# Attention and MLP in one kernel: merged exps and mask products, global rows added up by TensorE, and one opening order in place of two

## The chip, the cores and the metric

The kernel runs on one core of one Trainium2 chip. The metric is the device time of one execution in microseconds. Five engines work side by side, each through its own instructions in program order: TensorE (PE, matmuls; PEld, its weight loads), VectorE (DVE), ScalarE (ACT), GpSimd (POOL) and SyncE (SP). Matmul results go to PSUM, eight banks of 2 KB a partition. GpSimd and SyncE start the transfers (DMAs).

## The reference, cut to what matters

```python
def _attn_ref(q, k, v, global_idx):            # 8 batches, 8 heads, 576 tokens, head size 64
    scores = scale * np.matmul(q, k.transpose(0, 1, 3, 2))
    mask = np.abs(pos[:, None] - pos[None, :]) <= 32       # a band of 65
    mask = mask | is_global[:, None] | is_global[None, :]  # 8 global tokens
    attn = softmax(np.where(mask, scores, -1e9))
    return np.matmul(attn, v)

def _moe_ref(x, w_in, w_out):                  # 4608 tokens, 512 wide, 2048 inner
    h = x @ w_in
    g = h * np.cos(h)
    return g @ w_out
```

The attention's output, heads side by side, is x of the second part.

## The kernel before

**The work.** Heads go in pairs: 32 pairs, four to a batch of 576 tokens. A pair is worked off in steps, each a letter and the pair's number. *k* and *q* turn the natural rows of keys and queries with 16 small TensorE transposes (L618) and copy them to SBUF on ScalarE (L627, L638, L639); pairs 0 to 3 also pick the global columns with 16 matmuls (L323, copied at L324), and from pair 2 on the q step issues two filler matmuls first (L613). *s*, the scores, are ten matmuls (L654) into four PSUM banks, exps on ScalarE (L657, L661) and products with the mask on VectorE (L658, L662). *p*, the values, are 20 matmuls (L669) into the tile pv, then on VectorE the sum of the global rows' denominators (L683), two reciprocals (L684, L685) and the product xn (L689). *x* turns xn back with five transposes (L701) into xT, the MLP's input (L702, L705, L707); the last pair of a batch also has GpSimd copy the eight global columns to places held in registers (L710).

Pairs 0 to 9 go by five blocks of 120 tokens as above (scores5, values5, turn_x5); from pair 10 on another layout with eleven blocks is used (L722 to L775), with keys and queries cast to a 16-bit copy in DRAM and read back by a transposing DMA.

The MLP goes by nine tiles of 512 tokens. mlp_in makes one of 16 column blocks of h in four matmuls (L788), then a cos on ScalarE (L794) and a product on VectorE (L795); mlp_out adds four of its blocks into the output (L892); the last three tiles use a form with seven products in place of eight (L852). exp and cos need different function tables, so ScalarE loads a table whenever it changes between them.

**The order** is written out by hand in strings, one token a step. FRONT is the start, MID what follows it, then one string for each two pairs (FIFTH, SIXTH, ORDER) and TAIL. `1` is an mlp_in with its cos, `m` one without, `t` a cos alone, `2` an mlp_out. `w4` are four filler matmuls (L330) and `f8` eight (L514). GpSimd's queue has: `L` load of keys and queries of four heads (L290), `W` one of four chunks of w_in (L993), `O` w_out (L997), `C` cast of four heads' values (L423), `E` and `A` gathers of the global rows (L346), `H` turning them, `g` copying them into a pair's keys and queries (L598, L605), `I` the iotas and the loads of the eight positions into registers (L1045 to L1048), `K` the casts to DRAM (L277, L281). SyncE's queue has `M`, the loads of four heads' values (L384, L389), and `B`, the transposing reads (L295, L296). `y` makes the values' global rows (L430, copied at L431), `n` squares an output for a check (L914), `Z` is a part of the second layout's mask (L446 to L480), `N` holds GpSimd's queue until the mask is there. `+` and `-` say whether mlp_in may use the score banks. L1 stands for pairs 2 and 3, L2 for 4 and 5, and so on; so do C and M.

**PSUM.** pv has two banks, tag h two (turned rows, mlp_in), tag s three (scores, turned outputs), tag o one (the fourth score bank, mlp_out).

Of the kernel before, what the change touches and what calls it, by code (L numbers as in the profile page):

```python
# [53 lines left out]
MID = ("+ 1 1 1 1 Z0 1 1 1 Z5 B5 1 Z1 1 1 Z2 1 1 A0 1 Z3 1 1 A1 1 n0 A2 g10 g11 1 Z4 N K6 1 1 1 1 1 1 1 2 2 kc qc n1 2 2 1 1 B6 2 2 n2 kd qd - 2 2")  # L54
# [5 lines left out]
FRONT = ("M1 s0 E0 C0 E1 L2 w6 k1 q1 L3 w4 s1 M2 M3 y0.0 f8 k2 q2 C1 H0 I p0 y0.1 s2 k3 q3 x0 p1 H1 s3 g4 g5 g6 L4 C2 g7 k4 q4 x1 p2 M4 s4 "  # L60
         "k5 q5 x2 p3 s5 g8 g9 C3 W0 W1 W2 W3 k6 q6 x3 p4 s6 C4 k7 q7 x4 p5 s7 k8 q8 x5 p6 s8 H2 O k9 q9 p7 x6 s9 "
         "x7 p8 m m x8 K5 p9 t t + m m t t x9 -")
# [149 lines left out]
def kernel(  # L212
# [28 lines left out]
    gidx_row = const.tile([1, 2 * G], I32)  # L241
# [4 lines left out]
    nc.sync.dma_start(gidx_row, dview(gi, 0, (2 * G, 1), (1, 2 * G)))  # L246
# [7 lines left out]
    xT = keep.tile([P, NC, NT + 40], FP16)  # L254

# [70 lines left out]
    def warm(n, tag="s"):  # L326

        t = ps.tile([P, 4, P], FP32, tag=tag, bufs=2 + (tag == "s"))
        for _ in range(n):
            nc.tensor.matmul(t, ones16, view(ones16, (0, 4), (1, P)), start=True, stop=True)  # L330
# [76 lines left out]

    def hold_mask(_):

        nc.gpsimd.tensor_copy(gate, mask[0:1, 0, 0:1])  # L410
# [8 lines left out]
    def cast_vn(s):  # L419
        if s == 2:  # L420
            nc.gpsimd.tensor_copy(gate, pm_of[max(pm_of)][0:1, 2 * CN - 1 : 2 * CN])
# [3 lines left out]
    def value_rows(s, part):  # L425

        hs = slice(2 * part, 2 * part + 2)
        rows = ps.tile([P, 512], FP32, tag="h", bufs=2, name="rows")
# [143 lines left out]
    def turn_globals(half, both):  # L572
        t = ps.tile([P, 2, 16 * G], FP16, tag="s" if half else "h", bufs=2 + half)
# [35 lines left out]
    def turned(src, pr, n, ahead=0):  # L609

        bank = ps.tile([P, 512], FP32, tag="h", bufs=2, name="bank")
        for _ in range(ahead):
            nc.tensor.matmul(bank, ones16, view(ones16, (0, 4), (1, P)), start=True, stop=True)  # L613
        t = view(bank.bitcast(FP16), (QP, RW), (1, QP))
# [4 lines left out]
        return t, bank[:, 400 : 400 + G]  # L619
# [24 lines left out]
    def scores5(pr):  # L644
        kp, qp = k5(pr), qb[pr % NK].rearrange("p j c -> p (j c)")
        pm = pm_of[pr] = work.tile([P, 2 * CN], FP16, tag="pm", name="pm")
        tags = (("s", 3), ("s", 3), ("s", 3), ("o", 1))
        st = [ps.tile([P, 512], FP32, tag=tag, bufs=bufs, name="st") for tag, bufs in tags]
        for t in (0, 1, 4, 2, 3):
            i, c = (0, OFF[t]) if OFF[t] < CA else (2, OFF[t] - CA)  # L650
            q0 = 0 if t == 0 else P * t - D
            for h in range(2):
                hp = slice(h * D, (h + 1) * D)
                nc.tensor.matmul(st[i + h][:, c : c + WID[t]], kp[hp, t], qp[hp, q0 : q0 + WID[t]], start=True, stop=True)  # L654
        for h in range(2):
            e = work.tile([P, 2 * CB], FP16, tag="e", bufs=3)
            nc.scalar.activation(e[:, 0:CA], st[h][:, 0:CA], AF.Exp, scale=scale)  # L657
            nc.vector.tensor_tensor(pm[:, h * CN : h * CN + CA], e[:, 0:CA], mask5[:, 0:CA], ALU.mult)  # L658
        e = work.tile([P, 2 * CB], FP16, tag="e", bufs=3)
        for h in range(2):  # L660
            nc.scalar.activation(e[:, h * CB : (h + 1) * CB], st[2 + h][:, 0:CB], AF.Exp, scale=scale)  # L661
        nc.vector.tensor_tensor(view(pm[:, CA:], (CN, 2), (1, CB)), view(e, (CB, 2), (1, CB)), view(mask5[:, CA:], (0, 2), (1, CB)), ALU.mult)  # L662

    def values5(pr):
# [13 lines left out]
        for h in range(2):  # L678
            add(h, 0, P, G, 1, 0, False, True)
        den = pv[:, :, D : D + 1]  # L680
        rp = r_all[:, pr]
        dg = work.tile([G, 2], FP32, tag="dg")
        nc.vector.tensor_reduce(dg, view(pv[0:G, :, X + D : X + D + 1], (512, 2), (X, 4)), AX.X, ALU.add)  # L683
        nc.vector.reciprocal(view(rp, (NK5, 2), (1, NK5)), view(den, (512, 2), (X, NK5)))  # L684
        nc.vector.reciprocal(view(rp[0:G, 1:], (NK5, 2), (1, 4)), view(dg, (1, 2), (0, 4)))  # L685
# [508 lines left out]
```

## Time and profile before

| what | value |
|---|---|
| time, median of 3 runs | 336.7 us (336.4 to 339.61) |
| span of the profiled execution | 335.3 us |
| the profiled execution's own time | not listed beside its span |
| TensorE busy | 322.3 us (96%) |
| VectorE, ScalarE, GpSimd busy | 269.7, 241.1, 107.6 us |
| pair 10's scores begin (end of FRONT and MID) | 82.78 us |

The span is counted from the first to the last instruction. In the rows of the profile a line starts with the start and the length in us, then the engine, the line of the kernel, the operation, output <- inputs, shapes and a count; in brackets stands how long the engine had been idle and what released it. Grouped rows have busy us and mean ns after the bar.

### The profile page before, as it was taken

The numbers are of one execution on the slowest core, as the hardware profiler recorded it, in microseconds if no ns is written. First come the engines' busy times: TensorE is split into PE (matmuls) and PEld (weight loads), VectorE is DVE, ScalarE is ACT, GpSimd is POOL, SyncE is SP. The second block draws the span as 40 slices with busy tenths as digits, with TensorE's granted clock in tenths as the row PEclk, the third lists the DMA queues.
The fourth block names the chain that finished last, engine by engine and source line by source line (L and its number), as shares of the span: only waits on it lengthen the run. The fifth ranks groups of instructions, "written<-read, shape, count | busy, mean of one in ns | idle before, by whom it ended". The sixth has DMA issues, their size and how long they took to land.

```text
span 335.3 us, 8640 instructions
## 1 busy us (share of the span) xinstructions
PE 322.3 (96%) x3269; PEld 180.1 (54%) x3269; DVE 269.7 (80%) x649; ACT 241.1 (72%) x422; POOL 107.6 (32%) x216
## 2 busy tenths in 40 slices
PE   7999889999999999999999999999999999999992
PEld 3566654444545454545454545454545566666781
DVE  6778889984679798989898989898989878778771
ACT  4788886785958887777778787878787865665710
POOL 7856578361071407241623252325000200000000
PEclk9999999999999999999999999999999999999997
DMA  5999899999999999999999999999990010100212
GB/s 72 213 179 208 152 205 199 194 133 164 138 179 153 150 161 145 201 155 170 147 195 147 164 149 183 135 178 141 194 109 34 32 33 31 65 32 0 96 47 88
DMA packets 167220, 45.01 MB, mean 134 GB/s; under 512 B 153108, under 2 KB 163732, under 8 KB 166996
## 3 DMA queue, kind: packets, MB, share of 16 engines
q1 hardware_dynamic: 107556, 26.73, 55.9%
q0 software_dynamic: 59472, 17.54, 51.0%
q8 instruction: 27, 0.44, 0.6%
q14 instruction: 21, 0.17, 0.2%
q10 hardware_dynamic: 144, 0.13, 0.1%
HBM read 44.93 MB, written 19.17 MB: 191 GB/s over the span
## 4 chain that ended last, share of the span: by engine, by line
PE 84%; DVE 7%; ACT 5%; issue 2%; ACTq 0%; DVEq 0%
PE ph L788 29%; PE po L892 23%; PE wx L852 6%; PE wy L852 5%; PE units L788 4%; PE pv L742 3%; PE t L330 3%; PE st L722 3%; DVE g L795 2%; PE pv L669 2%; PE tx L767 2%; PE bank L618 2%; PE st L654 1%; ACT cos L794 1%; PE bank L613 1%
## 5 line engine op out<-in xcount | busy, mean ns | idle before, releaser
L788 PE MATMUL ph<-xT,w_in 128*128 128x512 f16 x512 | 123.3, 379 | 0.5 <-DVE xg L707 0.2
L794 ACT ACTIVATE cos<-ph,pio 128x512 f16<-128x512 f32 x128 | 86.5, 687 | 41.5 <-PE ph L788 39.4
L795 DVE TENSOR_TENSOR g<-cos,ph 128x512 f16<-128x512 f16 x128 | 85.6, 684 | 17.9 <-ACT cos L794 15.9
L892 PE MATMUL po<-w_out,g 128*128 128x512 f16 x384 | 93.5, 379 | 0.0
L788 PEld LDWEIGHTS <-w_in 128*128 128x128 f16 x576 | 53.8, 98 | 57.7 <-issue 1.5
L892 PEld LDWEIGHTS <-g 128*128 128x128 f16 x384 | 36.6, 98 | 43.1
L725 ACT ACTIVATE e<-st 128x512 f16<-128x512 f32 x44 | 23.9, 594 | 8.2 <-PE st L722 8.1
L726 DVE TENSOR_TENSOR pm<-e,mask 128x512 f16<-128x512 f16 x44 | 18.8, 428 | 13.4 <-ACT e L725 12.1
L1079 POOL COPY gate<-xn 1x1 f16<-1x1 f16 x8 | 1.4, 179 | 81.0 <-DVE xn L753 81.0
L775 POOL COPY xT<-xg 128x4 f16 x48 | 15.8, 328 | 32.2 <-DVE xT L770 29.6
L281 POOL DMA_DIRECT2D q<-in_q_dram x11 | 24.3, 2206 | 0.0
L753 DVE TENSOR_TENSOR xn<-pv,r_all 128x768 f16<-128x768 f32 x22 | 21.1, 958 | 0.7
L852 PEld LDWEIGHTS <-g 128*128 128x128 f16 x192 | 18.7, 98 | 5.2
L914 ACT ACTIVATE xn<-xn 128x1536 f16<-128x1536 f16 (+1 forms) x15 | 21.2, 1411 | 0.0
L281 POOL DMA_DIRECT2D k<-in_k_dram x11 | 18.0, 1638 | 1.4 <-issue 1.4
L794 ACT ACTIVATE cos<-units,pio 128x512 f16<-128x512 f32 x16 | 11.0, 689 | 9.8 <-PE units L788 9.6
L795 DVE TENSOR_TENSOR g<-cos,units 128x512 f16<-128x512 f16 x16 | 11.0, 686 | 7.4 <-ACT cos L794 7.3
L788 PE MATMUL units<-xT,w_in 128*128 128x512 f16 x64 | 16.4, 379 | 0.0
L794 ACT ACT_TABLE_LOAD x12 | 15.4, 1283 | 0.2
L600 POOL COPY kw<-kgT 128x88 f16<-128x88 f16 x22 | 14.6, 884 | 0.0
L725 ACT ACT_TABLE_LOAD x11 | 14.1, 1283 | 0.2
L722 PEld LDWEIGHTS <-kw 64*128 64x128 f16 x484 | 8.4, 95 | 10.2 <-issue 8.4
(215 smaller groups left out, 500.1 us busy)
## 6 DMA issues: line engine op xcount, KB each, us to landing
out_dram<-o SPq DMA_DIRECT2D x24, 256.0 KB
vw<-v SPq DMA_DIRECT2D x32, 165.0 KB
k<-in_k_dram POOLq DMA_DIRECT2D x11, 288.0 KB, 8.1
q<-in_q_dram POOLq DMA_DIRECT2D x11, 288.0 KB, 11.0
v<-in_v_dram POOLq DMA_DIRECT2D x11, 288.0 KB, 5.4
vn<-in_v_dram SPq DMA_DIRECT2D x20, 120.0 KB
w_in<-in_moe_w_in_dram POOLq DMA_DIRECT2D x4, 512.0 KB, 10.1
w_out<-in_moe_w_out_dram POOLq DMA_DIRECT2D x1, 2048.0 KB, 17.8
```

The lines of the kernel that those rows point to most:

```text
L281: nc.gpsimd.dma_start(dst[s].rearrange("t (h d) -> t h d", h=4), dview(src, base, (D, S), (S * D, 4), (1, D)))
L722: nc.tensor.matmul(st[j // 8 * 2 + h][:, j % 8 * C : j % 8 * C + C], kp[hp, j], qp[hp, j], start=True, stop=True)
L725: nc.scalar.activation(e[:, 0:512], st[h], AF.Exp, scale=scale)
L726: nc.vector.tensor_tensor(view(pm[:, h], (1, 512)), e[:, 0:512], view(mask, (1, 512)), ALU.mult)
L753: nc.vector.tensor_tensor(view(xn, (384, 2), (D, 6), (1, D)), view(pv, (512, 2), (65, 6), (1, D)), view(rp, (6, 2), (1, 6), (0, D)), ALU.mult)
L775: nc.gpsimd.tensor_copy(xT[:, :, bass.ds(pool_idx[g] + b * S, 1)], xg[:, :, g : g + 1])
L788: nc.tensor.matmul(ph, w_in16[:, j, f * P : (f + 1) * P], xT[:, j, t * TT : (t + 1) * TT], start=(j == 0), stop=(j == NC - 1))
L794: nc.scalar.activation(cos, ph, AF.Sin, bias=pio2)
L795: nc.vector.tensor_tensor(g, cos, ph, ALU.mult)
L852: nc.tensor.matmul(bank[:, a], left(f)[:, a * P : a * P + P], right(f), start=name in "125" and f == 0 and (split or a == 0), stop=f == HF ...
L892: nc.tensor.matmul(po, g16[:, f, s * P : (s + 1) * P], w_out16[:, f], start=(f == 0), stop=(f == NF - 1))
L914: nc.scalar.activation(view(xn, (BP * P, 2), (1, n)), view(xn, (BP * P, 2), (1, n)), AF.Square, accum_out=x_sq[:, s : s + 1])
```

## The change

- In pairs 0 to 9 the scores of both heads go to the two banks of one double tile; one exp and one mask product take both heads. Four exps become two, three products two. The four score banks are two double tiles until `F` in the order, then three banks s and one o as before; any step that asks for an s or o bank before `F` takes a whole double tile.
- values5 adds the global rows of all blocks into one place with eight small matmuls (8 rows each) instead of two, so the sum of denominators and the second reciprocal go, and the sum in turn_x5 becomes a copy.
- FRONT and MID become one string, OPEN. k is turned earlier than its q in many pairs, ahead of the scores of the pair before. The register loads and mask parts Z0 to Z4 stand at the start, the later gathers A0 to A2 and w_in chunks 1 and 0 among the first pairs, chunks 2 and 3 about pairs 5 and 6; the last two value products and four outputs stand among the mlp_in. The filler matmuls are 13 + 4 + 2 + 4, before 13 + 4 + 4 + 6 + 4. The counts of `1` with `m` (30) and `2` (8) are the same.
- The registers are loaded from gidx_all, so gidx_row and its transfer go. A few tiles share room; `finish_check` gains a memset; cos takes its bias as a constant.

```diff
-FRONT = ("M1 s0 E0 C0 E1 L2 w6 k1 q1 L3 w4 s1 M2 M3 y0.0 f8 k2 q2 C1 H0 I p0 y0.1 s2 k3 q3 x0 p1 H1 s3 g4 g5 g6 L4 C2 g7 k4 q4 x1 p2 M4 s4 "
-         "k5 q5 x2 p3 s5 g8 g9 C3 W0 W1 W2 W3 k6 q6 x3 p4 s6 C4 k7 q7 x4 p5 s7 k8 q8 x5 p6 s8 H2 O k9 q9 p7 x6 s9 "
-         "x7 p8 m m x8 K5 p9 t t + m m t t x9 -")
-MID = ("+ 1 1 1 1 Z0 1 1 1 Z5 B5 1 Z1 1 1 Z2 1 1 A0 1 Z3 1 1 A1 1 n0 A2 g10 g11 1 Z4 N K6 1 1 1 1 1 1 1 2 2 kc qc n1 2 2 1 1 B6 2 2 n2 kd qd - 2 2")
+OPEN = ("w2 M1 I Z0 R1 E0 C0 E1 L2 Z1 M2 k1 Z2 H2 M3 s0 P0 f8 Z3 q1 s1 Z4 k2 y0.0 w4 W1 C1 H0 k3 L3 q2 p0 - A0 y0.1 "
+        "s2 q3 x0 W0 p1 s3 H1 R2 k4 g4 g7 p2 g6 q4 k5 p3 g5 x1 s4 A1 Q8 C2 L4 q5 g8 k6 M4 A2 x2.1 s5 g9 W2 q6 C3 x3 "
+        "W3 p4 s6 q7 g10 k7 + x4.1 O C4 K5 p5 k8 s7 g11 k9 q8 p6 x5.1 q9 s8 p7 s9 n0 m F m K6 x6.1 Z5 1 t 1 p8 1 1 1 "
+        "1 1 B5 1 x7.1 1 p9 1 2 t 1 N0 1 n1 + m t 2 1 1 2 x8.1 1 k10 1 m n2 2 1 q10 2 2 k11 1 1 q11 1 t 1 1 1 2 x9 1 "
+        "1 B6 2 1 -")
...
+    def two_banks():
+
+        return rooms[1].tile([P, 2, 512], FP32, tag="a", bufs=2, name="two")
...
 def scores5(pr):
-        tags = (("s", 3), ("s", 3), ("s", 3), ("o", 1))
-        st = [ps.tile([P, 512], FP32, tag=tag, bufs=bufs, name="st") for tag, bufs in tags]
+        both = front[0]
+        st = [two_banks(), two_banks()] if both else [[bank("s") for _ in range(2)], [bank("s"), bank("h")]]
...
-        for h in range(2):
-            e = work.tile([P, 2 * CB], FP16, tag="e", bufs=3)
-            nc.scalar.activation(e[:, 0:CA], st[h][:, 0:CA], AF.Exp, scale=scale)
-            nc.vector.tensor_tensor(pm[:, h * CN : h * CN + CA], e[:, 0:CA], mask5[:, 0:CA], ALU.mult)
...
+        for i, c, n in ((0, 0, CA), (1, CA, CB)):
+            e = work.tile([P, 2 * CA], FP16, tag="e", bufs=3)
+            if both:
+                nc.scalar.activation(view(e, (n, 2), (1, n)), st[i][:, :, 0:n], AF.Exp, scale=scale)
...
+            nc.vector.tensor_tensor(view(pm[:, c:], (CN, 2), (1, n)), view(e, (n, 2), (1, n)), view(mask5[:, c:], (0, 2), (1, n)), ALU.mult)
 def values5(pr):
-        for h in range(2):
-            add(h, 0, P, G, 1, 0, False, True)
+        for t in (4, 2, 3, 0):
+            for h in range(2):
+                add(h, t, D if t else P, G, 1, 0, False, t == 0)
...
-        dg = work.tile([G, 2], FP32, tag="dg")
-        nc.vector.tensor_reduce(dg, view(pv[0:G, :, X + D : X + D + 1], (512, 2), (X, 4)), AX.X, ALU.add)
         nc.vector.reciprocal(view(rp, (NK5, 2), (1, NK5)), view(den, (512, 2), (X, NK5)))
-        nc.vector.reciprocal(view(rp[0:G, 1:], (NK5, 2), (1, 4)), view(dg, (1, 2), (0, 4)))
 def turn_x5(pr, tag="s"):
-            nc.vector.tensor_reduce(xg[:, p], view(tx[:, 1], (1, G), (P, 4)), AX.X, ALU.add)
+        nc.vector.tensor_copy(xg[:, p], tx[:, 1, 0:G])
...
         build_mask5()
         local_k(0)
-        warm(4)
         local_q(0)
         warm(4)
...
-                gidx_row[0:1, 0 : 2 * G : 2], engines=[mybir.EngineType.Pool], min_val=0, max_val=S - 1)[1])
+                gidx_all[0:1, 0 : 2 * G : 2], engines=[mybir.EngineType.Pool], min_val=0, max_val=S - 1)[1])
```

In OPEN, `R` says how many MLP tiles may be begun, `Q` how many mlp_out may be issued, `P0` holds GpSimd's queue until pair 0's product is there, `x4.1` takes a double tile (after `F` an s bank) for the turned output instead of an h bank.

140 lines of the change are left out of this document (79 added, 61 removed).

## The prediction

> **What bounds the kernel now.** First the page's part 1, then busy time in windows cut at 45.4 (ninth pair scored), 82.8 (pair 10 scored, where the hand-written opening ends) and 104 us.
>
> ```profile
> PE 322.3 (96%) x3269; PEld 180.1 (54%) x3269; DVE 269.7 (80%) x649; ACT 241.1 (72%) x422; POOL 107.6 (32%) x216
> 7.40:45.40 38.00, 35.47 (x798) 24.89 (x797) 30.56 (x105) 30.44 (x77) 26.56 (x49) 1.00 1.12 191
> 45.40:82.80 37.40, 36.55 (x209) 17.04 (x211) 31.12 (x81) 26.93 (x41) 19.17 (x31) 1.00 1.50 177
> 104.00:252.00 148.00, 148.00 (x1470) 75.12 (x1469) 127.94 (x282) 116.39 (x192) 47.40 (x96) 1.00 1.49 159
> ```
>
> The columns are busy us and count of TensorE, its weight loads, VectorE, ScalarE and GpSimd, then the granted clock, the DMA share and GB/s. From 104 to 252 us TensorE is busy for 148.00 of 148.00. The steps there stay, so a gain must make pair 10's scores start before 82.78. What TensorE does until then:
>
> ```profile
> 8.03 1.04 PE L330 MATMUL t<-ones 128*128 128x512 f16 x4
> 9.00 0.47 PE L618 MATMUL bank<-ident,room 76*64 76x76 f16 x16
> 9.30 0.39 PE L323 MATMUL bank<-one_q,room 76*64 76x8 f16 x16
> 9.63 1.04 PE L330 MATMUL t<-ones 128*128 128x512 f16 x4
> 10.61 0.55 PE L654 MATMUL st<-qb,kw 64*128 64x136 f16 x10
> ...
> 14.75 0.55 PE L654 MATMUL st<-qb,kw 64*128 64x136 f16 x10
> ...
> 26.51 1.03 PE L669 MATMUL pv<-vw,pm 128*128 128x65 f16 x20
> 27.48 0.55 PE L654 MATMUL st<-qb,kw 64*128 64x136 f16 x10
> 27.95 0.47 PE L618 MATMUL bank<-ident,w_out 75*64 75x75 f16 x16
> 28.36 0.61 PE L613 MATMUL bank<-ones 128*128 128x512 f16 x2
> 28.89 0.47 PE L618 MATMUL bank<-ident,w_out 76*64 76x76 f16 x16
> 29.29 0.45 PE L701 MATMUL tx<-ident,xn 128*128 128x128 f16 x5
> 29.58 1.03 PE L669 MATMUL pv<-vw,pm 128*128 128x65 f16 x20
> 30.99 0.55 PE L654 MATMUL st<-qb,kw 64*128 64x136 f16 x10 [0.38 <-issue]
> ...
> 44.84 0.55 PE L654 MATMUL st<-qb,kw 64*128 64x136 f16 x10 [0.19 <-ACT qb L639]
> ...
> 52.90 21.31 PE L788 MATMUL ph<-xT,w_in 128*128 128x512 f16 x96
> 74.05 3.62 PE L892 MATMUL po<-w_out,g 128*128 128x512 f16 x16
> ...
> 82.78 0.41 PE L722 MATMUL st<-qb,kw 64*128 64x64 f16 x16
> ```
>
> Start to start a pair costs: values 0.97, scores 0.47, k turned 0.41, two fillers 0.53, q turned 0.40, output turned 0.29. Pairs 0 to 3 add a pick of 0.33 to k and to q (9.30 to 9.63). A group of four MLP matmuls takes 21.15/24 = 0.88. A filler of L330 takes (10.61-9.63)/4 = 0.24.
>
> Work from 7.40 to the ninth score's end at 45.33: 20 turnings 8.1, picks 2.6, 16 fillers of L613 4.2, scores 4.7, eight value products 7.8, seven outputs 2.0, 18 fillers of L330 4.4 and about 1.8 of small things (value rows, fill, globals): 35.6. **2.3 us are waits.** From there to 82.78 both kernels issue 30 groups of mlp_in and 8 of mlp_out (38 x 0.88 = 33.5) with two value products and three outputs, 36.3 of 37.45: **1.15 us of waits.** So 3.45 us of waits and 4.4 of fillers is all there is to win. The waits at 30.99 and after have one shape:
>
> ```profile
> 31.39 1.05 ACT L657 ACTIVATE e<-st 128x488 f16<-128x488 f32 x2 [0.50 <-PE st L654]
> 32.33 0.88 ACT L661 ACTIVATE e<-st 128x384 f16<-128x384 f32 x2
> 33.07 0.69 ACT L627 COPY kw<-bank 128x600 f16<-128x600 f16 x1
> 33.61 0.22 ACT L638 COPY qb<-bank 128x8 f16<-128x8 f16 x1
> 33.66 0.73 ACT L639 COPY qb<-bank 128x600 f16<-128x600 f16 x1
> 34.84 1.04 ACT L657 ACTIVATE e<-st 128x488 f16<-128x488 f32 x2 [0.45 <-PE st L654]
> ```
>
> ScalarE goes 0.94 + 0.74 for exps, 0.54 k copy, 0.78 q copy; TensorE waits for the q copy, then ScalarE 0.45 for the scores: 3.45 a pair.
>
> **The change, part by part.** *Merged exps and products.* Two exps of 488 columns start 0.94 apart from what follows: 0.96 ns a column, almost no fixed part left to save. I take 0.06 us a pair for ScalarE (bounds: 0, and 0.3 were every overlap lost). The products wait for both heads, 0.45 later; the value product comes at least three TensorE steps later and hides it. On VectorE:
>
> ```profile
> L685 DVE RECIPROCAL r_all<-dg 8x8 f32<-8x8 f32 x10 | 1.9, 191 | 0.3
> L683 DVE TENSOR_REDUCE dg<-pv 8x2 f32<-8x8 f32 x10 | 1.5, 149 | 2.3 <-PE pv L669 2.2
> ```
>
> The sum and second reciprocal go, 0.34 a pair on an engine busy 30.56 of 38: worth nothing unless TensorE waits for xn.
>
> *Global rows on TensorE.* Six more value matmuls a pair, 60 in all, 8 weight columns by 65. From below the 8-column picks: 0.33/16 = 21 ns; from above the mean of today's value matmuls, 0.97/20 = 48 ns. I take 23 ns, the nearer row being the small one: 0.14 a pair, **+1.4 us** (1.2 to 2.9), none hidden since TensorE is the bound.
>
> *Fillers.* 8 of 31 go: **-1.9 us** of TensorE, if nothing else makes it stand there.
>
> *The order.* I lay the new order out by hand, each engine in sequence, with the steps above. q0 starts at 9.00 as before, after a 0.9 wait that four fillers used to cover. k1 now stands ahead of score 0, so its copy goes ahead of exp 0, which starts near 12.5 instead of 11.01 (0.41 after the score's start). q1's copy follows exp 0 at 14.2 to 15.0, and score 1 comes at 15.0 (14.75 before); TensorE stands 1.2 there, having only q1 to do. Score 3 comes at 24.5, score 4 at 29.5 against 27.48, with p3 and k5 (1.5) already behind it. Score 5 waits for q5's copy behind exp 4, 0.8; scores 6 and 7 come without a wait, which is the gain that turning k ahead brings. Score 9 needs both double banks, and waits 0.75 for exp 8 of the ninth pair: it ends at 45.9, with one output less done. New waits until there 3.7. Then two MLP groups, output 6, two groups and p8 fill 5 us, while ScalarE does exp 9, the squares of n0 (1.4), a table load (1.3) and the first cos; the fifth group waits 0.6 for a bank. From 46.5 there remain 38 x 0.88 + 4 x 0.29 + 2 x 1.1 = 36.8, so 83.3 for pair 10 without any load late. As a sum: fillers -1.9, waits -3.45 + 4.3, value matmuls +1.4, and 0.4 for w_out (below): **+0.75**.
>
> *What moves on GpSimd and the queues.* The later gathers (A0 to A2) and two w_in chunks come ahead of loads and casts that were ahead of them.
>
> ```profile
> 10.48 1.02 POOL L346 DMA_INDIRECT kg<-in_k_dram,gidx_rows  x1 [0.30 <-DMA vn<-in_v_dram]
> 11.81 1.10 POOL L346 DMA_INDIRECT kg<-in_k_dram,gidx_rows  x1 [0.30 <-issue]
> ...
> 20.32 1.25 POOL L423 CAST vw<-vn 128x1280 f16<-128x1280 f32 x1 [0.94 <-DVE r_all L685]
> ...
> 25.25 0.37 POOL L598 COPY kw<-kgT 128x40 f16<-128x40 f16 x1 [2.62 <-ACT e L657]
> ...
> 36.94 1.43 POOL L423 CAST vw<-vn 128x1280 f16<-128x1280 f32 x1 [3.83 <-DMA vn<-vg]
> 38.31 3.00 POOL L993 DMA_DIRECT2D w_in<-in_moe_w_in_dram  x4
> ...
> 63.58 0.95 POOL L346 DMA_INDIRECT vg<-in_v_dram,gidx_rows  x1 [4.21 <-DMA w_out<-in_moe_w_out_dram]
> w_out<-in_q_dram POOLq DMA_DIRECT2D x1, 320.0 KB, 6.8
> ```
>
> The last row is a transfer's: size, then us from issue to landing. A gather of two takes 2 x 1.33, a cast 1.25, a chunk's issue or another load's 0.75; the global copies at 0.43 a pair are an estimate from the 0.37 at 25.25. The register loads do not show; they lie inside the idle 2.62, so cost 0 to 2.6, and I take 1, most of that idle being a wait for the turned globals. From C1 at 20.3: C1, H0, L3 to 23.8; A0, W0 to 27.2; four global copies to 28.8; A1, C2 to 32.7; L4 to 34.1; g8, A2, g9, W2 to 38.4; C3 39.8; three more and O to 44.5; C4 46. TensorE wants p4 (C2) at 34.3, q8 (L4's second part, issued 33.4, landing 6.8 later) at 40, p6 (C3) at 40.9, p8 (C4) at 49.7. It just fits, with 1.1 us in hand at p6 and none at q8; this thin cover makes the range's upper half. The same bytes stand ahead of w_out as now. It landed at 63.58 (a gather waited for it); without the dip quoted below, worth about 2 us at 200 GB/s, and one or two smaller, it lands at 60.3 to 61.4. The first mlp_out stands at 46.5 + 13.4 = 59.9, against 74.05 now: a wait of 0.4 to 1.5, and I take 0.4. The mask parts (some 3.7 on VectorE) move into the first pairs, where it is busy 6 of 10 us: nothing.
>
> **The rivals.** *Loads late (slower).* From 7.4 to 45.4 us the queues carry 191 GB/s on the mean (last column of the first window above), with one dip:
>
> ```profile
> 36.00:38.00 2.00, 1.64 (x44) 1.39 (x41) 1.63 (x7) 1.84 (x5) 1.06 (x1) 1.00 0.59 128
> ```
>
> Two chunks of 0.52 MB put 5.2 us of traffic before the value loads that C3 waits for, which landed at 36.94. An earlier start on SP (about 1.5) works against it: 40.6, C3 done at 42.0, TensorE waits 1.1 at p6; if SP gets the worse of it, 42.1 and 2.6, and with register loads at their upper bound L4 adds 1.5. So 338.5 to 341.5, deciding once C3 ends after 40.9. Against it: L4 no longer competes early. The Trainium skill, "DMA: Bandwidth & Descriptors", section "Queues, rings and completion order", says that each DMA engine takes turns between queue rows packet by packet; by that rule the small value packets would lose bytes to the w_in rows. The row above shows SP's queue alone, not the split, so no trace here shows it. Chance 0.20.
>
> *Waits gone (faster).* If k1 lands earlier and the double banks come free in time, the waits of 1.2, 0.8, 0.75 and 0.6 vanish: 0.75 - 3.35 = -2.6, 334.1; with the 8-column matmuls hidden behind larger weight loads another 1.4, 332.7. For it: VectorE loses 0.34 a pair. Against: ScalarE's order as written. Chance 0.28, since my waits come from a chain of many small steps and each could be one that the engines overlap.
>
> *The clock falls.* The first 13 matmuls take 0.44 each, later ones 0.24; the fillers kept TensorE busy.
>
> ```profile
> 1.79 5.68 PE L330 MATMUL t<-ones 128*128 128x512 f16 x13 [1.79 <-DVE pio L1004]
> ```
>
> If the new waits of 0.9 and 1.2 brought that pace back for the next 3.5 us, it would cost about 1.7: 339.1. The Trainium skill, "TensorE: Matmul & The Clock Gate", Part 1, says the clock halves after an idle window of about 3.4 us; no wait here is as long, and the granted clock reads 1.00 in every window above. Chance 0.05.
>
> *No effect*, every wait replaced one for one, lies inside the forecast.
>
> **How the numbers follow.** The profiled span is 335.3; the execution's own time is not listed, and the median shown, 336.7, is 1.4 above the span, which I take as what lies around it. 335.3 + 0.75 + 1.4 = **337.4**. Chances: forecast 0.47 (335.7 to 339.1), waits gone 0.28, loads late 0.20, clock 0.05. The range takes in the fast rival with its cheap matmuls below, and above the dearer end of the value matmuls (+1.5) with the middle of the late loads (+1.9): 332.7 to 340.8. One per cent, 3.4 us, is about what a measurement of this kernel can tell from no change. Faster by more needs the fast rival with part of its cheap matmuls (0.18); slower needs the upper part of late loads or two bad cases together (0.13); 0.69 lies between.
>
> **What would show it.** Score 0's exp near 12.5 and score 1 near 15; a q copy directly behind exp 4; ninth score ending at 45 to 47; the first cos about 4.5 after it; pair 10's scores at 82.5 to 84; value products 1.1 apart from the next step. If pair 10 starts by 80, my waits are wrong; if GpSimd's C3 waits for vn past 40, the loads decide. After pair 10 I count on no change; if that stretch moves by over 0.5 us, the forecast is wrong for a reason not named here.

## The result, and the profile after

The changed kernel takes **349.0 us** (median of 4 runs, 347.4 to 353.6) against 336.7 (336.4 to 339.6): ratio 1.033, interval 1.029 to 1.038. The forecast was 337.4 with a range to 340.8: a change that could hardly be told from none was forecast, and 3.3% more time was measured, 11.6 us above the forecast. The profiled execution took 348.4 with a span of 346.7. Ratios here leave out executions over 1.5% above the fastest of their kernel; where that matters (one kernel below) both groups are given.

First the page of the kernel after, parts 1, 2 and 4: busy time of the engines, the granted clock in 40 slices, and the shares of the chain that ended last. The last row is the chain of the kernel before.

```profile
PE 327.0 (94%) x3321; PEld 183.3 (53%) x3321; DVE 268.8 (78%) x620; ACT 227.4 (66%) x402; POOL 107.9 (31%) x216
PEclk9999699999899999999999999999999999999999
PE 69%; DMA 17%; ACT 4%; SPq 3%; POOL 2%; DVE 2%; issue 2%; POOLq 0%; ACTq 0%
...
PE 84%; DVE 7%; ACT 5%; issue 2%; ACTq 0%; DVEq 0%
```

TensorE's work is 4.7 us longer (322.3 before), the span 11.4. So 6.7 of the 11.4 us are standing still, and two slices of the clock (the fifth and the eleventh, about 35 to 43 and 87 to 95 us) are clearly below full. Transfers hold 17% of the chain, where the kernel before shows none.

TensorE's timeline of the kernel after, the steps that the prediction named (start, us, line, operation, and in brackets the idle time before it and what ended it):

```profile
14.96 0.55 PE L679 MATMUL two<-qb,kw 64*128 64x136 f16 x10 [1.30 <-ACT qb L663]
24.09 0.55 PE L679 MATMUL two<-qb,kw 64*128 64x136 f16 x10
29.13 1.19 PE L694 MATMUL pv<-vw,pm 128*128 128x65 f16 x25 [0.84 <-issue]
32.66 0.47 PE L642 MATMUL bank<-ident,room 75*64 75x75 f16 x16 [0.54 <-DMA room<-in_k_dram]
35.00 0.50 PE L679 MATMUL two<-qb,kw 64*128 64x192 f16 x4 [1.14 <-DVE xg L729]
37.55 1.92 PE L694 MATMUL pv<-vw,pm 128*128 128x65 f16 x26
...
50.05 0.84 PE L679 MATMUL two<-qb,kw 64*128 64x136 f16 x10
...
86.22 4.30 PE L809 MATMUL bank<-xT,w_in 128*128 128x512 f16 x12 [4.43 <-DVE g L816]
95.04 0.49 PE L743 MATMUL bank<-qb,kw 64*128 64x64 f16 x22
```

Up to score 3 (24.09; forecast 24.5) the kernel follows the sum. Score 4 stands at 30.64 (29.5). Then 0.84, 0.54 and 1.14 us of waits follow each other, and the value products at 37.55 take 1.92 instead of 1.2. Score 9 ends at 50.9 instead of 45.9, 5.5 us behind the kernel before. From there to pair 10 another 6.8 us are lost, 4.4 of them in the one wait at 86.22. Pair 10 comes at 95.04, 12.3 us late. Behind it 251.7 us are left, against 252.5.

The windows of the kernel after say what happened to the products:

```profile
34.00:36.00 2.00, 1.00 (x6) 0.27 (x6) 1.59 (x5) 1.33 (x2) 1.83 (x5) 0.69 1.16 185
36.00:38.00 2.00, 2.00 (x30) 1.52 (x29) 0.76 (x2) 1.08 (x3) 1.70 (x2) 0.50 1.22 232
38.00:40.00 2.00, 2.00 (x32) 1.66 (x31) 0.86 (x5) 0.00 (x0) 1.26 (x4) 0.50 1.20 198
40.00:42.00 2.00, 2.00 (x38) 0.92 (x34) 1.50 (x3) 1.80 (x4) 0.00 (x0) 0.60 1.20 195
80.00:90.00 10.00, 5.40 (x18) 2.01 (x17) 5.08 (x10) 2.35 (x5) 0.00 (x0) 0.83 0.89 87
```

The granted clock (third from the end) was 0.50 from 36 to 40 us. The loss of clock from 34 to 42 is 0.31 x 2 + 0.5 x 4 + 0.4 x 2 = 3.4 us at most. In the last window TensorE is busy for 5.40 of 10.

GpSimd and VectorE. The first row is of the kernel before, the rest of the kernel after:

```profile
71.42 1.71 POOL L281 DMA_DIRECT2D k<-in_k_dram  x1 [0.61 <-issue]
...
44.10 1.26 POOL L447 CAST vw<-vn 128x1280 f16<-128x1280 f32 x1 [4.83 <-DMA vn<-in_v_dram]
...
51.67 1.60 POOL L303 DMA_DIRECT2D k<-in_k_dram  x1
...
54.78 2.68 POOL L303 DMA_DIRECT2D k<-in_k_dram  x1
...
78.39 0.54 DVE L654 COPY kw<-kT 128x1320 f16<-128x1320 f16 x1 [3.46 <-DMA kT<-k]
84.66 0.47 DVE L666 COPY qb<-qT 128x616 f16<-128x616 f16 x1 [3.95 <-DMA qT<-q]
```

C3 ended at 45.4, where 39.8 was forecast and 40.9 was the point from which the late loads decide. The two rows of L303 are the first transfers of K5 and K6, the casts of the fifth and the sixth double pair: before, K6 was issued at 71.4, behind the hold `N`; now it follows K5, at 54.8. From 65 to 75 us, when the keys and queries of pair 10 are read back (issued at 67.29 and 69.21), the DMA share is 2.05; in the kernel below that holds K6 back it is 1.34. VectorE then stands 3.5 and 4.0 us for the transposed keys and queries of pair 10, with mlp products queued behind those copies, and TensorE waits for these products (86.22). **The prediction never priced the move of K6.**

### The profile page after: what moved, and what is told of

It reads as the page before. It is cut to its first block, busy times and chain, and to the rows that moved or that the text cites. A ratio compares the mean times of both kernels' runs of the same rounds, so it can differ in the third digit from the quotient of the medians.

```text
span 346.7 us, 8677 instructions
## 1 busy us (share of the span) xinstructions
PE 327.0 (94%) x3321; PEld 183.3 (53%) x3321; DVE 268.8 (78%) x620; ACT 227.4 (66%) x402; POOL 107.9 (31%) x216
## 4 chain that ended last, share of the span: by engine, by line
PE 69%; DMA 17%; ACT 4%; SPq 3%; POOL 2%; DVE 2%; issue 2%; POOLq 0%; ACTq 0%
PE bank L809 26%; PE bank L913 19%; PE bank L873 11%; DMA vn<-in_v_dram 5%; DMA w_out<-in_moe_w_out_dram 5%; DMA qT<-q 4%; PE units L809 4%; PE pv L763 3%; PE bank L743 2%; PE bank L788 2%; DMA room<-in_q_dram 2%; DMA vw<-vg 2%; SPq L459 1%; SPq L411 1%; SPq L390 1%
## 5 line engine op out<-in xcount | busy, mean ns | idle before, releaser
L809 PE MATMUL bank<-xT,w_in 128*128 128x512 f16 x512 | 126.0, 383 | 4.9 <-DVE g L816 4.6
L815 ACT ACTIVATE cos<-bank 128x512 f16<-128x512 f32 x128 | 75.0, 596 | 59.3 <-PE bank L809 53.2
L816 DVE TENSOR_TENSOR g<-cos,bank 128x512 f16<-128x512 f16 x128 | 86.1, 685 | 22.5 <-ACT cos L815 19.8
L913 PE MATMUL bank<-w_out,g 128*128 128x512 f16 x384 | 94.3, 379 | 0.2 <-DMA w_out<-in_moe_w_out_dram 0.2
L746 ACT ACTIVATE e<-bank 128x512 f16<-128x512 f32 x44 | 23.9, 596 | 8.9 <-PE bank L743 8.8
L303 POOL DMA_DIRECT2D q<-in_q_dram x11 | 24.9, 2264 | 0.0
L683 ACT ACTIVATE e<-two 128x976 f16<-128x976 f32 (+1 forms) x20 | 17.0, 898 | 5.7 <-PE two L679 5.7
L303 POOL DMA_DIRECT2D k<-in_k_dram x11 | 19.0, 1726 | 0.5 <-issue 0.5
L687 DVE TENSOR_TENSOR pm<-e,qT 128x976 f16<-128x976 f16 (+1 forms) x20 | 14.2, 732 | 4.5 <-ACT e L683 3.4
L815 ACT ACTIVATE cos<-units 128x512 f16<-128x512 f32 x16 | 9.6, 598 | 11.4 <-PE units L809 11.1
L694 PE MATMUL pv<-vw,pm 128*128 128x65 f16 (+3 forms) x260 | 13.1, 201 | 2.0 <-issue 0.8
```

What stands on the lines that cost most here:

```text
L303: nc.gpsimd.dma_start(dst[s].rearrange("t (h d) -> t h d", h=4), dview(src, base, (D, S), (S * D, 4), (1, D)))
L683: nc.scalar.activation(view(e, (n, 2), (1, n)), st[i][:, :, 0:n], AF.Exp, scale=scale)
L746: nc.scalar.activation(e[:, 0:512], st[h], AF.Exp, scale=scale)
L809: nc.tensor.matmul(ph, w_in16[:, j, f * P : (f + 1) * P], xT[:, j, t * TT : (t + 1) * TT], start=(j == 0), stop=(j == NC - 1))
L815: nc.scalar.activation(cos, ph, AF.Sin, bias=pi / 2.0)
L816: nc.vector.tensor_tensor(g, cos, ph, ALU.mult)
```

## The experiments

The theory after the traces: the new order costs the time, not the new instructions, by K6's traffic, by w_in chunks ahead of the value loads, and by small waits behind which the clock falls. The diffs are cut to the tokens that move.

**The order or the instructions.** All new instructions, with the strings of the kernel before:

```diff
-OPEN = ("w2 M1 I Z0 R1 E0 C0 E1 L2 Z1 M2 k1 Z2 H2 M3 s0 P0 f8 ...")
+OPEN = ("R1 " + old FRONT + " F R2 Q8 " + old MID)      # x0.1 to x5.1, x8.1, x9.1
         local_k(0)
+        warm(4)
         local_q(0)
```

> The new instructions with the old order: merged exps and mask products, the global rows summed by TensorE, two double banks in the front, the constant bias of the cosine, the value products twice per pair; but the order of the steps is that of the kernel before (register loads, mask parts, w_in chunks, casts and the second warm-up at their old places, the casts of the sixth double pair behind their hold), with the transposed steps of the front in single banks. Theory that the new order and the casts set free cause the loss: 335 to 338 us, with the first score of pair 10 at 82 to 84 us. Rival, that the new instructions cause it (merged exps release the banks later, longer products share VectorE with GpSimd's casts, more TensorE time for the values): 341 us or more, and the ninth score ends at 47 us or later. A value between would say that both have a share.

Where the expectation speaks of single banks, the edit does something else: x0 to x5, x8 and x9 take a double tile (`.1`) where they had an s bank before.

Measured 337.1 us against 337.3 for the kernel before, ratio 0.998 (0.995 to 1.002). In sum the new instructions cost nothing that can be measured and gain nothing; the loss comes with the order. TensorE's timeline of this kernel:

```profile
45.13 0.55 PE L675 MATMUL two<-qb,kw 64*128 64x136 f16 x10
...
83.77 0.41 PE L739 MATMUL bank<-qb,kw 64*128 64x64 f16 x16
```

Score 9 stands 0.3 and pair 10 starts 1.0 later than before; the stretch behind it (span 334.4) is 250.6, 1.9 shorter (the section on why says where).

**K6 held**, on the kernel after (`V10` holds GpSimd's queue until pair 10's queries are copied):

```diff
-... s9 n0 m F m K6 x6.1 Z5 ... k11 1 1 q11
+... s9 n0 m F m x6.1 Z5 ... k11 V10 K6 1 1 q11
```

> The change as it is, but GpSimd's casts of the sixth double pair are issued behind the sixth double pair's twelfth query step and only once the query of pair 10 has been copied, not directly behind the casts before them. Theory: in the kernel after, those casts (POOL 54.78 to 59.6 us) let the loads behind them start early, and their traffic delays the transposed reads of pair 10 (DVE waits 3.46 us for kT and 3.95 us for qT); TensorE's 4.43 us wait at 86.22 and the slow matmuls behind it (12 in 4.13 us) should go, about 6 us: 343 us, and the first score of pair 10 near 89 us instead of 95.04. Rival: the transposed reads are late because all of the front is 5.5 us late; then nothing changes here, 348 to 349.5 us, with kT and qT landing no earlier than 78 and 84 us.

Measured 342.7 us, ratio 1.019 (1.015 to 1.022): 6.3 us less by the medians and 5.0 by the ratios, as the theory said. VectorE and TensorE of this kernel:

```profile
74.80 0.53 DVE L654 COPY kw<-kT 128x1320 f16<-128x1320 f16 x1
77.39 0.47 DVE L666 COPY qb<-qT 128x616 f16<-128x616 f16 x1
...
88.42 0.49 PE L743 MATMUL bank<-qb,kw 64*128 64x64 f16 x22
```

Neither copy waits any more, and pair 10 starts at 88.42 (89 expected). The front is still late, and its timeline holds a surprise, since its instructions up to 50 us are those of the kernel after:

```profile
14.97 0.55 PE L679 MATMUL two<-qb,kw 64*128 64x136 f16 x10 [1.30 <-ACT qb L663]
...
26.77 1.92 PE L694 MATMUL pv<-vw,pm 128*128 128x65 f16 x26
28.62 0.91 PE L679 MATMUL two<-qb,kw 64*128 64x136 f16 x10
```

Score 1 stands where it stood, but the granted clock falls to 0.50 right behind it, the products at 26.77 go at half the pace, and score 3 comes at 28.62 instead of 24.09. The same instructions lost the clock some 18 us earlier. Where it falls differs from run to run.

**w_in later**, on the kernel after:

```diff
-... y0.0 w4 W1 C1 ... q3 x0 W0 p1 ... s5 g9 W2 q6 C3 x3 W3
+... y0.0 w4 C1 ... q3 x0 p1 ... s5 g9 q6 C3 W0 W1 W2 x3 W3
```

> The change as it is, but the first three chunks of w_in are loaded behind the cast C3, as in the kernel before, instead of in pairs 0, 1 and 5. Theory that the early w_in loads hold back the values: C3 goes from 44.10 us to under 40, w_out's load is issued and lands about 4 us earlier, the twelfth transposed step waits less for its input rows (0.54 us), and the ninth score ends 1 to 3 us before 50.83: 346 to 348 us. Rival, that the order of the steps on TensorE and VectorE sets the front: the ninth score ends at 50 to 51 as in the kernel after and the time stays 348 to 350, since TensorE waited for values only 0.5 us in the front; C3 may still move.

Measured 345.9 us, ratio 1.024 (1.019 to 1.029), 3.1 us by the medians. GpSimd's cast C3 in this kernel:

```profile
38.40 1.28 POOL L447 CAST vw<-vn 128x1280 f16<-128x1280 f32 x1
```

C3 comes 5.7 us earlier, so the chunks do hold back the values. Score 9 ends at 49.7, 1.2 earlier only, and pair 10 comes 1.7 earlier. The profiled execution is the slowest of the four (346.8), so where the others gained more is not shown.

**The turned output of pair 2 in a single bank**, on the kernel after (`x2.1` becomes `x2`):

> The change as it is, but the transposed step of pair 2 puts its result into a single bank instead of one of the two double banks. Theory: that step holds a double bank, so the score of pair 5 waits 1.14 us at 35.00 for VectorE's copy of it, and the granted clock falls behind that wait (0.69 in 34 to 36, 0.50 in 36 to 38 us), which costs some 3 us more: the ninth score ends near 47 instead of 50.83 and the time is 345 to 346.5. Rival: the clock falls for the sum of the small waits before (0.84 at 29.13, 0.54 at 32.66), so only the 1.1 us goes: 347.5 to 348.5 us. No effect, if the wait moves to the next bank: 348.5 to 350.

Measured 349.3 us, ratio 1.037 (1.032 to 1.042): no effect, though the wait ahead of score 5 was gone and score 6 came at 37.2 instead of 39.4. TensorE's timeline shows what took its place:

```profile
46.88 1.87 PE L694 MATMUL pv<-vw,pm 128*128 128x65 f16 x26 [2.94 <-POOL vw L447]
```

Once the front was in time, p6 waited 2.94 us for C3, which came at 45.57, and the clock was at 0.50 behind it. In the kernel after this wait does not show: C3 was done at 45.4, and TensorE came to p6 only at 45.70. A wait that the trace doesn't show can stand right behind the one that it does.

**One part alone, in the kernel before.** K6 behind K5:

```diff
-... x8 K5 p9 ...  Z4 N K6 1
+... x8 K5 K6 p9 ...  Z4 N 1
```

> The kernel before with one thing changed: GpSimd's casts of the sixth double pair directly behind those of the fifth, as in the kernel after, instead of behind the hold on the mask. Theory that the early casts alone cost their 6 us: their loads and the reads behind them queue ahead of the transposed reads of pair 10, TensorE waits some 4 us before pair 10, and the time is 341 to 343 us. Rival, that the casts hurt only because the front of the kernel after is 5.5 us late and w_out's load with it: 336.5 to 338 us, pair 10 still first scored near 83 us.

Measured 340.4 against 338.8 us, ratio 1.007 (1.004 to 1.011): 2.4 us by the ratio. That lies between the 4 to 6 us of the theory and the 1 us or less of the rival, so neither holds. TensorE at score 9 and VectorE of this kernel:

```profile
50.09 0.55 PE L654 MATMUL st<-qb,kw 64*128 64x136 f16 x10
...
81.33 0.53 DVE L630 COPY kw<-kT 128x1320 f16<-128x1320 f16 x1
```

The copy of kT comes 5.8 us later than before (75.57) and does not wait. But in this execution the clock was at 0.50 from 20 to 30 us, and score 9 already stands 5.2 us late (44.84 before), so the copy had been put off by the front and says nothing of the traffic. What the 2.4 us of the other executions are is not shown. In this order K6 costs less than in the new one, and it is not free.

**w_in early, in the kernel before** (W1, W0 and W2 at the places of the new order):

> The kernel before with one thing changed: three chunks of w_in are loaded where the kernel after loads them, two of them in pairs 0 and 2 and one in pair 5. Theory that they hold back the values: the fourth cast of the values goes from 36.94 to 41 us or later (38.40 to 44.10 is what the kernel after shows against the one with late chunks), TensorE and its granted clock wait for it, and the time is 339 to 342 us. Rival, that the cast has 4 us of room in the old order too: 336.5 to 338 us, with the cast later all the same.

Measured 347.3 against 338.8 us, ratio 1.029 (1.018 to 1.040): 6 to 13 us, more than any theory gave. GpSimd, first C2 in the kernel before and then in this one, and TensorE of this one:

```profile
30.51 1.25 POOL L423 CAST vw<-vn 128x1280 f16<-128x1280 f32 x1 [2.16 <-DMA vn<-in_v_dram]
...
40.13 1.25 POOL L423 CAST vw<-vn 128x1280 f16<-128x1280 f32 x1 [8.49 <-DMA vn<-in_v_dram]
...
41.44 1.54 PE L669 MATMUL pv<-vw,pm 128*128 128x65 f16 x20 [3.20 <-POOL vw L423]
```

C2 waits 8.49 us for its values and starts at 40.13 instead of 30.51. TensorE waits 3.20 for it at p4. The granted clock is 0.50 already from 20 to 32 us, ahead of that wait, and 0.50 to 0.70 again from 40 to 48 behind it, so how much of the loss is the late values alone is not shown.

**The three edits together**, and then **with ten fillers**:

```diff
         local_k(0)
+        warm(4, "h")
         local_q(0)
 ...
-... Z3 q1 s1 Z4 ...
+... Z3 q1 w6 s1 Z4 ...
```

> The change with the three edits of the runs before together: casts of the sixth double pair held until the query of pair 10 is copied, w_in chunks behind C3, the transposed step of pair 2 in a single bank. Theory: the casts (6.3 us) and the values (3.1 us) add up, and the third edit gives its 1.1 us once the values no longer end last: 338 to 340.5 us if the granted clock falls once more in the front (2 to 5 us of it), 336 to 338 if not. Rival, that the two gains overlap (both bring w_out and the reads of pair 10 forward): 341 to 343 us.

> The kernel of the three edits with the filler matmuls of the old front restored: four behind the first key step, as in the kernel before, and six ahead of the score of pair 1, where TensorE waits 1.30 us in the kernel after. They compute nothing that is used. Theory that the small waits of the first 16 us let the granted clock fall (to 0.50 for 2 to 12 us, at another place in each run): the clock stays at 1.00 to 20 us at least and the time is 1 to 4 us below that of the kernel without the fillers: 335.5 to 338 us. Rival, that the clock falls all the same behind later waits (1 us ones at 32 to 37 us), or that the fillers delay the steps by as much as they save: within 1 us of the kernel without them.

Measured 346.0 us both, ratios 1.024 (1.017 to 1.032) and 1.026 (1.016 to 1.035). Both theories missed, and of the rivals only the one that the fillers change nothing came true: the gains did not add up, not even to the 341 to 343 us of overlapping ones. Score 9 ended only at 56.3 and 56.5 us. Score 1, at 14.96 in the kernel after, already stands at 18.55 and 18.98, behind waits of 3.36 and 2.23 us for ScalarE's copy of q1. And ScalarE of the kernel of three edits shows a wait that the openings of the other kernels' profiled runs do not have:

```profile
25.98 0.19 ACT L346 CAST kw<-bank 128x40 f16<-128x40 f32 x1 [3.92 <-remote]
```

The one with fillers has 2.65 us of it at nearly the same time (25.93), the one without a further 1.35 at 17.68. In both, a packet of the instruction queue q14 falls into the half microsecond from 24.0 or 23.5. That ScalarE waited there for its next instructions fits, but was not tried. These two ran on another chip than the first four kernels, so how much of the 346 us is due to these waits stays open.

**The gathers** A0 to A2, with the copies g10 and g11 that need them, put back into the mlp stretch, with K6 held and w_in late:

```diff
-... p0 - A0 y0.1 ... s4 A1 Q8 C2 ... M4 A2 x2.1 ... Z5 1 t 1 p8 1 1 1 1 1 B5 1 x7.1 1 p9
+... p0 - y0.1 ... s4 Q8 C2 ... M4 x2.1 ... Z5 1 t 1 A0 p8 1 1 A1 1 1 1 B5 1 x7.1 A2 1 g10 p9
```

> The change with the casts of the sixth double pair held and the w_in chunks behind C3 (as in the kernel of three edits), and with the six indirect gathers of the later global rows, A0 to A2, and the two steps g10 and g11 that need them put back into the mlp stretch, where the kernel before has them. Theory that the gathers in the front are the next cause, because they stand in GpSimd's and the software queue ahead of C2 and C3 (two of them at 29.93 to 32.16 us in the kernel after, just ahead of C2, two at 35.81 to 38.14 ahead of C3): the ninth score ends at 46 to 48 us and the time is 338 to 340.5. Rival, that the waits of the first 20 us and the granted clock behind them make the front late: the ninth score ends at 50 to 56 and the time stays 342 to 346.

Four executions: 337.7 and 338.7 us at a mean clock of 0.999 and 0.991, 345.2 twice at 0.965 and 0.972. The ratio 1.001 (0.995 to 1.007) is of the former alone. With these three moves undone the kernel is as fast as before, in the executions that keep the clock. The profiled execution is one of the latter (clock 0.50 from 16 to 36 us), so its trace does not show the front of a quick one. The share of the gathers is not shown either: the kernel with three edits and the gathers early took 346.0 at clocks of 0.975 to 0.981, this one 345.2 where it lost the clock.

**The gathers early in the old order**, with the new instructions (A0 behind p0, A1 ahead of C2, A2 behind M4):

> The new instructions in the old order (which took the time of the kernel before), with one thing of the new order: the six indirect gathers A0 to A2 in the front, at the kernel after's places. Theory that the gathers hold GpSimd's casts of the values: C2 goes from 29.99 to 32 us or later and C3 from 36.49 to 39 or later, TensorE waits for it, 338.5 to 341 us. Rival, that the old order has the room for them: within 1 us of the old order alone, 336 to 338 us.

Measured 336.4 against 337.6 us, ratio 0.997 (0.993 to 1.002): no cost that can be measured. The rival holds.

**The early part alone**, in the old order with the new instructions (register loads, row numbers, mask parts, queries one step later, eight filler matmuls less):

> The new instructions in the old order, with the first part of the new order up to the products of pair 1: the register loads, row numbers and mask parts in the first 15 us, the queries of pairs 1 to 3 one step later, no filler matmuls between the first key and the first query. The w_in chunks and the gathers stay at their old places. Theory that this part alone costs by its waits and the granted clock (TensorE waits 1.30 us ahead of the score of pair 1 and is idle 2.2 of 8 us before it in the kernel after): 338.5 to 342 us, with a clock of 0.5 somewhere before 30 us. Rival, that it gains what it was meant for, since the mask parts leave the mlp stretch: 334.5 to 336.5 us.

Measured 339.1 against 337.6 us, ratio 1.003 (0.999 to 1.008): 1.1 us, not told from none. The median lies in the theory's range, and as it said the clock falls before 30 us: it is 0.63 and 0.52 from 16 to 20 us, behind the same wait of 1.30 at score 1. What was to be gained by the mask parts did not appear.

**Fillers against the fall of the clock**, on the kernel with the gathers back (the ten fillers above):

> The kernel with the casts held, the w_in chunks behind C3 and the gathers put back (337.7 and 338.7 us where the granted clock was 0.999 and 0.991, 345.2 twice where it was 0.965 and 0.972), with ten filler matmuls: four behind the first key step, as the kernel before has them, and six ahead of the score of pair 1. They compute nothing that is used. Theory that the small waits of the first 16 us let the granted clock fall in some executions: with fillers in them all executions have a clock over 0.985 and take 337 to 340 us. Rival, that the clock falls behind waits later in the front or by chance: executions near 345 us stay.

Measured 337.2 against 336.9 us, ratio 0.999 (0.996 to 1.002). All ten executions have a clock of 0.992 or more and take 335.8 to 338.8; none is near 345. So the register loads, the mask parts and the keys turned ahead stay where the change put them, and the time is that of the kernel before. In its profiled execution score 9 starts at 46.57 and ends at 47.4 (forecast 45.9), and pair 10 starts at 85.67. The same two windows in four kernels, in this order: before, after, K6 held, gathers back with fillers.

```profile
8.00:16.00 8.00, 7.93 (x151) 4.58 (x147) 5.84 (x24) 5.70 (x16) 6.92 (x8) 1.00 1.26 218
16.00:28.00 12.00, 11.10 (x281) 8.29 (x280) 8.90 (x30) 9.71 (x27) 8.43 (x18) 1.00 1.14 192
```

```profile
8.00:16.00 8.00, 5.82 (x172) 4.30 (x166) 7.34 (x33) 5.24 (x13) 6.37 (x10) 1.00 1.19 223
16.00:28.00 12.00, 11.36 (x279) 8.24 (x273) 8.91 (x21) 9.14 (x21) 11.39 (x14) 1.00 0.92 167
```

```profile
8.00:16.00 8.00, 5.67 (x162) 4.23 (x162) 7.34 (x34) 5.10 (x13) 6.53 (x10) 1.00 1.19 222
16.00:28.00 12.00, 12.00 (x183) 8.14 (x177) 5.57 (x13) 6.91 (x16) 11.39 (x14) 0.53 0.90 156
```

```profile
8.00:16.00 8.00, 7.74 (x172) 4.82 (x170) 7.34 (x33) 5.11 (x13) 6.49 (x9) 1.00 1.20 220
16.00:28.00 12.00, 10.72 (x251) 7.56 (x246) 8.42 (x21) 9.10 (x19) 8.60 (x17) 1.00 0.94 171
```

TensorE is busy 7.93 of 8 us, then 5.82, 5.67 and 7.74; with 5.67 the clock behind it is 0.53. With 5.82 it held until 34.

**K6 early again**, in the kernel with the gathers back and no fillers:

> The kernel with the w_in chunks behind C3 and the gathers put back, but with the casts of the sixth double pair early again, as in the kernel after. Theory that their 6 us in the kernel after are their own: 343 us or more at a full clock (338.2 with the casts held), TensorE waiting some 4 us for the transposed reads of pair 10. Rival, that they cost what they cost in the old order alone (2.4 us), and the rest came from the late front of the kernel after: 340 to 341.5 us at a full clock.

Measured 343.9 us, ratio 1.019 (1.016 to 1.022); the three executions with a clock over 0.99 take 343.2 to 344.4. Against 337.7 and 338.7 with K6 held, K6 so costs 5 to 6 us of its own in the new order, at a full clock and with the values in time. VectorE and TensorE, in the one execution that lost the clock (0.971):

```profile
80.44 0.54 DVE L654 COPY kw<-kT 128x1320 f16<-128x1320 f16 x1 [3.27 <-DMA kT<-k]
...
85.69 2.75 PE L809 MATMUL bank<-xT,w_in 128*128 128x512 f16 x12 [1.85 <-DVE g L816]
```

**Two candidates**, from the new instructions in the old order with the gathers early. First the turned output of pair 9 in a single bank (`x9.1` becomes `x9`), then also VectorE's sums of the global rows as before:

> A candidate: the new instructions in the old order with the gathers A0 to A2 in the front (336.4 us), and the last transposed step of the front in a single bank, because TensorE waits 1.13 us there at 54.03 us for VectorE to read a double bank out. Theory: that wait goes, 335 to 336 us, ratio about 0.994. Rival: the single bank is one that the mlp groups use, and the wait moves to them: 336 to 337.5 us.

> The kernel of the last candidate (new instructions in the old order, gathers early, 336.6 us) with one part taken back: the global rows are summed by VectorE again (a reduction and a second reciprocal of the denominators, a reduction of the transposed rows) instead of by six more TensorE value products per pair. Theory: the value products are the one part that costs TensorE time (0.19 us for each of ten pairs, 1.9 us in the front, by the spacing of the value products), the front ends 1.5 to 2 us earlier, the gain behind pair 10 stays: 334.5 to 335.5 us. Rival, that VectorE's reductions come back as waits of the transposed steps and of the scores, as in the kernel before: 336 to 337 us.

Measured 336.6 us, ratio 0.999 (0.997 to 1.001), and 337.7 us, ratio 1.001 (0.998 to 1.004). Both times the rival holds, in that neither differs from the kernel before: the 1.13 us came back as 0.16 and 0.69 at the next mlp groups, and the 1.9 us of value products as waits of 0.2 to 0.7 for VectorE. No version beat the kernel before by more than can be measured.

## Why the prediction was wrong, step by step

- *Fillers, -1.9.* The time left TensorE but nothing took its place: 5.82 of 8 us busy where there were 7.93. Putting ten fillers into the kernel with the gathers back cost nothing (337.2 against 337.7 and 338.7) and all executions kept the clock. The sum put nothing against this gain for the clock; only the clock rival did.
- *Waits until score 9, +3.7 in the front.* Right in place up to score 3 (1.30 at score 1 for 1.2). Behind it waits of 0.84, 0.54 and 1.14 came that I had not laid out: one inside a run of value products, with no releaser in the profile, one for L3's keys, one for VectorE, whose products of pair 4 took 2.35 us beside a cast (last section). With the clock behind them score 9 ends 5.0 us later than laid out.
- *Waits gone, chance 0.28.* No: the 1.2 at score 1 was there with 1.30. The 0.8 at score 5 came as 1.14, but for VectorE to read a double tile out, not for q5's copy, so that its size was near is luck. The 0.75 at score 9 was not there: score 8 waited 0.16 for a double tile, score 9 for none.
- *The clock, chance 0.05.* This step failed in its reason: "no wait here is as long". From 7 to 34 us the longest wait was 1.30, and the clock fell to 0.50. I had taken one rule of the Trainium skill, "TensorE: Matmul & The Clock Gate", Part 1, on an idle window of about 3.4 us, as the bound. The same page of the Trainium skill tells, under "A second HAM failure mode: psum-queue depth-cycling", of another kernel in which frequent short idle spells between groups of matmuls let the clock go back and forth; the windows above agree in that no long wait was needed. The price forecast, 1.7, was half of the 3.4 that the windows of the kernel after give as a bound.
- *Loads late, chance 0.20.* The mechanism and its mark were right: C3 waited for vn past 40 (to 44.10). Its size was not. I gave 5.2 us of traffic less an earlier start of 1.5; alone in the old order the chunks moved C2 by 9.6 us and the time by 6 to 13. In the kernel after moving them back gains about 3 us; that it is not more because TensorE was late anyway is argued (with x2 in a single bank p6 did wait 2.94 us for C3) and not shown.
- *The missing term, and the step that failed most.* Under "What moves on GpSimd and the queues" I listed gathers, chunks and the casts of values, and left out K6, whose move from behind `N` at 71.4 to 54.8 us stands in the string. So the sum put it at nothing. It costs 5 to 6.3 us (5.0 and 6.3 taken out, 5 to 6 put in), about half the loss; the reads of pair 10 behind it (kT, qT) were never set against their landing.
- *Value products, +1.4.* The term was undersized: a pair goes from 0.97 to 1.15 or 1.16, six matmuls of 31 ns, 1.9 us in ten pairs, inside the range given (1.2 to 2.9). Taking them back gained nothing, since waits for VectorE took their place.
- *Merged exps, 0.06 a pair, and VectorE's sums, nothing.* From the first exp of a pair to the copy behind both, ScalarE goes from 1.68 to 1.57, so 0.11 a pair. The kernel with the old order bears out in sum that little hangs on these: ratio 0.998.
- *w_out, +0.4.* Measured 0.18, by luck: the first mlp_out came at 65.37 instead of 59.9 and w_out landed just before it, 4 to 5 us later than forecast.
- *After pair 10, no change.* 0.9 us less, and 1.9 in the old order, more than the 0.5 that I had set. The last group of matmuls starts as follows, in the kernel before, after, and with the old order:

```profile
326.81 1.91 PE L852 MATMUL wx<-xT,g 128*128 128x256 f16 x16
...
339.69 1.91 PE L873 MATMUL bank<-xT,g 128*128 128x256 f16 x16
...
327.54 1.91 PE L869 MATMUL bank<-xT,g 128*128 128x256 f16 x16
```

  From pair 10 to there it is 244.0, 244.7 and 243.8 us, so this part moved by +0.6 and -0.3. The rest, from there to the end of the span, is 8.5, 7.0 and 6.9 us. That end differs between runs of the same instructions behind pair 10: it is 8.0 and 7.2 in the two one-part kernels in the old order, whose other instructions are those of the kernel before. So the gain lies mostly or wholly in how the execution ends, and its reason is not shown. The cosine did get shorter, from the page of the kernel before, then after:

```profile
L794 ACT ACTIVATE cos<-ph,pio 128x512 f16<-128x512 f32 x128 | 86.5, 687 | 41.5 <-PE ph L788 39.4
```

```profile
L815 ACT ACTIVATE cos<-bank 128x512 f16<-128x512 f32 x128 | 75.0, 596 | 59.3 <-PE bank L809 53.2
```

  It takes 596 ns instead of 687 without the bias tile. It was in the diff and I gave it no term. TensorE sets the time there (busy 148.00 of 148.00 before), and ScalarE's idle time ahead of these cosines went up from 41.5 to 59.3 us. So no gain can be put down to the shorter cosine.

What stays open: how the other half of the loss is divided, beyond about 3 us for w_in, between the gathers, the small waits and the clock; and what exactly lets the clock fall. A busy share of TensorE does not decide it alone: in the profiled runs of both one-part kernels in the old order it was 7.71 and 7.70 of 8 us from 8 to 16, the waits ahead were 0.2 to 0.5 us long, and the clock fell to 0.50 at 20 us. The kernel before had mean clocks of 0.974 to 0.999 on the chips of these runs. Without fillers three of eight executions of the kernels with the gathers back lost the clock (two with K6 held, on another chip, and one with K6 early), with fillers none of ten. Of the profiled executions, all eight that open as the kernel after does, with no fillers put back, lost it somewhere before 40 us; of the nine with the fillers in place six kept it, and three lost it, the kernel of three edits with fillers among them (at 38 us). That points to the fillers and does not prove them.

## What to carry to other kernels

When a hand-written order is changed, list every moved token that issues a transfer and set it against the landing time of each transfer that is read soon after, not only against those of its own kind: here one group of casts, moved 17 us ahead, cost half the loss, and 2.4 us where the rest of the order stayed. Take fillers out only where other work fills their place: here the longest wait of a stretch did not tell whether the clock would hold. A part that gains nothing in the trace (a wait removed) may only have uncovered the next one in line, so undo parts from both sides: one alone in the old kernel, and one taken back in the new.

## What the runs showed of the hardware that was not expected

- The granted clock fell to 0.50 behind waits of 1.3 us and less: at 34 us in the kernel after, at 16 us in the one with K6 held, whose first 50 us have the same instructions, and at 20 us in the two one-part kernels in the old order.
- VectorE's fp16 product slows beside GpSimd's cast. The kernel after, VectorE and GpSimd, first two products beside a cast and then two without:

```profile
32.08 2.35 DVE L687 TENSOR_TENSOR pm<-e,qT 128x976 f16<-128x976 f16 x2
32.16 1.27 POOL L447 CAST vw<-vn 128x1280 f16<-128x1280 f32 x1
...
41.05 1.26 DVE L687 TENSOR_TENSOR pm<-e,qT 128x976 f16<-128x976 f16 x2 [0.46 <-ACT e L683]
```

  2.35 against 1.26, and 2.19 and 1.94 in the old order's kernel where a cast falls beside them (35.97 and 43.21). The Trainium skill, "Trainium Architecture — The Big Picture", "What this means for kernel authors", calls the port that the two share an exclusive lock; the 1.1 us more for a cast of 1.27 agree. So where a cast stands among the products is worth about a microsecond of VectorE.
